# A 96-byte pad among the constants of a transformer-block kernel

## The chip, the core and the metric

The kernel runs on one core of a Trainium2 chip. The core's engines work side by side and wait for each other through semaphores: TensorE (PE in the profile; its weight loads stand apart as PEld), VectorE (DVE), ScalarE (ACT), GpSimd (POOL) and SyncE (SP), which issues nearly all transfers. The metric is the time of one execution on the device, in microseconds (us). Three runs of the kernel before gave 955.26, 956.42 and 956.73 us, so the median is 956.42 us.

## What is computed

One block of a transformer with adaptive layer norms, on 2048 tokens of width 512: a sliding-window attention with 32 heads of width 16 and a window of 256, and then a gated feed-forward part (SwiGLU) of width 1792. Cut to what matters:

```
mod = (silu(c) @ w_mod).reshape(1, 6, 1, 512)        # sa, ca, ga, sb, cb, gb
h = layernorm(x) * (1 + ca) + sa
q, k, v = split(h @ wqkv)                            # 32 heads of 16
p = softmax(mask(q @ k.T * 16 ** -0.5), -1)          # 0 <= i - j < 256
x = x + ga * ((p @ v) @ wo)
h = layernorm(x) * (1 + cb) + sb
x = x + gb * ((silu(h @ w1) * (h @ w3)) @ w2)
```

All of it is float32 from outside. Inside, most matrix products are made of three products of a high and a low part (`hi*hi`, `hi*lo`, `lo*hi`) in the type `F32R`.

## The kernel before

The program is a list of instructions for each engine, set in order by a planner inside the kernel (class `Sched`) with tables of numbers. The change does not touch the planner or its tables.

The work runs in four stages, which overlap at their borders:

1. **Start, to about 92 us.** The layer norm of `x` is written, turned, as `hT`. Line 703 makes the values `vS` from it: `hT` is the stationary operand (the weights that are loaded into the array), `wvh` or `wvl` the moving one (that streams through it).
2. **Attention, to about 471 us**, in 32 units (8 groups of 4 heads, 4 blocks of 512 tokens). Line 518 projects queries and keys (stationary `wq`, moving `hT`), lines 574 and 931 make scores (both operands in `ring`), line 892 multiplies by the values (stationary `vS`, moving `pt`).
3. **Output projection, 468 to 519 us**, line 1315 (stationary `o` or `x1b`, moving `wo`), with the second layer norm.
4. **Feed-forward, 514 to 950 us.** There are 2 halves of the tokens and 7 pairs of column blocks, so 14 passes. In each, line 1579 makes 84 matmuls (two column blocks, seven products of six: stationary a slice of the pass's weights, moving a tile of `b`), and line 1673 makes 48 (eight tiles of six: stationary the gated activations, moving the `w2` weights). The passes take turns between two sets of weight tiles, `WT[0]` and `WT[1]` (the index `s` of line 1579).

Where a tile lies in SBUF is set by pools, which are stacks from two sides. The pools `cst`, `ap`, `p0`, `a2` and `fp` grow from the low addresses; this text calls their tiles the **left side**. The pools `a1`, `hp` and `xp` are opened with `side="right"` and grow downwards from the high end: the **right side**. `cst` is the first pool on the left, so what is added there moves everything that the left side allocates later.

The lines that decide which side an operand is on, for the feed-forward part (`fp` is a left pool, `xp` a right one, and the names of line 1647 are tiles of `a1`, on the right):

```
1343  BB[m, k] = [fp.tile([P, BT], F32R, name=f"b{m}{k}{part}") for part in range(2)]
1345  WT[0, n] = [fp.tile([P, 7 * PH], F32R, name=f"w{n}{part}") for part in range(2)]
1346  W2.extend(fp.tile([P, 2, D], F32R, name=f"w2{part}") for part in range(2))
1355  for n, name in enumerate(("wo", "o")):
1356      WT[1, n] = [slot(f"{name}{part}", F32R, (P, KC, D), "xp").rearrange("p k c -> p (k c)")
1357                  for part in range(2)]
1579  nc.tensor.matmul(ps(bk), WT[s, n][w][:, col], BB[t, k][r],
1647  hn, ln = (("wq00", "wq10"), ("wq01", "wq11"), ("qkr", "qk0"), ("qk1", "qk2"),
1648            ("e0", "e1"), ("e2", "wqr"))[2 * t + f + (2 if last and t else 0)]
1673  nc.tensor.matmul(ps(bk), tiles[hk + (h,)][:, i * P:(i + 1) * P],
1674                   w2_of(last, y, f), start=(m == 0), stop=(m == 5))
```

In the very last pass half of line 1673's stationary tiles are those of line 1648: `e0`, `e1`, `e2` (left) and `wqr` (right).

Matmuls of each kind, by the side of their operands:

| line | stationary | moving | matmuls | sides |
|---|---|---|---|---|
| 703 | `hT` | `wvh`, `wvl` | 192 | right, left |
| 518 | `wq` | `hT` | 384 | right, right |
| 574, 931 | `ring` | `ring` | 512 + 512 | left, left |
| 1315 | `o`, `x1b` | `wo` | 192 | right, right |
| 1579, even passes | `w` | `b` | 588 | left, left |
| 1579, odd passes | `wo`, `o` | `b` | 588 | right, left |
| 1673 | `wq`, `qk`, `qkr`, `wqr` | `w` (`w2`) | 652 | right, left |
| 1673, end | `e` | `w` | 20 | left, left |

Lines 892 (`vS`, `pt`) are left, left too. The slices that the matmuls take out of these tiles start a multiple of 512 bytes into them (those of `vS` excepted, whose rows are 68 bytes apart), so an operand starts at its tile's address modulo 128.

Of the kernel before, what the change touches and what calls it, by code (L numbers as in the profile page):

```python
# [8 lines left out]
F32 = mybir.dt.float32  # L9
# [9 lines left out]
P = 128  # L19
# [349 lines left out]
def block_kernel(ctx: ExitStack, tc: tile.TileContext, x, wqk, wv, wo, w13, w2, c, crow, wmod, wmodt, out):  # L369
    nc = tc.nc  # L370

    cst = ctx.enter_context(tc.tile_pool(name="cst", bufs=1))
# [19 lines left out]
                op=ALU.add, axis=mybir.AxisListType.XY)  # L392

    modc = cst.tile([P, 4, KC], F32, name="modc")

    o_dr = [drm.tile([NQ * P, BT], F32, name=f"o_dr{b}") for b in range(NB)]
    g_dr = drm.tile([2, D], F32, name="g_dr")
# [1412 lines left out]
```

## Time and profile before

| | |
|---|---|
| median of three runs | 956.42 us |
| profiled execution, its own time | 956.27 us |
| its span, first to last instruction | 954.6 us |
| outside the span | 1.67 us |
| feed-forward, first to last matmul | 513.6 to 949.9 us |
| share of the span that PE is busy | 98% |
| share of PE in the chain that ended last | 86% |
| mean granted clock of PE | 0.998 |

The span is what the profile's rows explain; the 1.67 us around it are added to every sum. A matmul's own duration in the profile overlaps the next one's, since matmuls are pipelined; what one costs in a stream is the **step**, the time from its start to the start of the next. The timeline of PE gives it: it merges neighbours of one kind ("x6") and tells where each group starts.

### The profile page before, as it was taken

How to read it: one execution, taken by the hardware profiler on the slowest of the kernel's cores; microseconds unless marked ns; L12 is line 12 of the kernel's file. 1: busy time of each engine (PE TensorE's matmuls, PEld its weight loads, DVE VectorE, ACT ScalarE, POOL GpSimd, SP SyncE). 2: the span in 40 equal slices, each digit the busy share in tenths (PEclk: the TensorE clock that was granted, in tenths of full speed). 3: DMA queues.
4: the chain of work that ended last, by engine and by line, in shares of the span. 5: the costliest groups of instructions: out<-in, count | busy, mean ns of one | idle time of the engine just before them, and what ended most of it. 6: DMA issues, size and time to landing. Idle time of an engine off the chain costs nothing.

```text
span 954.6 us, 17091 instructions
## 1 busy us (share of the span) xinstructions
PE 937.3 (98%) x5296; PEld 714.9 (75%) x5296; DVE 734.3 (77%) x2065; ACT 561.1 (59%) x1263; POOL 498.9 (52%) x721
## 2 busy tenths in 40 slices
PE   8999999999999999998999999999999999999998
PEld 4678777777777677775688788888888888888886
DVE  8884989898989898998468765666679766667555
ACT  6533878787878787876779833433456333433230
POOL 3230877787878686867544655444866222221320
PEclk9999999999999999999999999999999999999999
DMA  9521444444544444437893555466684421322002
GB/s 327 191 73 40 132 170 146 147 145 147 167 159 146 146 146 145 135 129 232 240 277 101 176 162 191 137 185 221 221 279 144 149 82 57 99 84 76 23 23 88
DMA packets 81561, 141.64 MB, mean 148 GB/s; under 512 B 10555, under 2 KB 23227, under 8 KB 81470
## 3 DMA queue, kind: packets, MB, share of 16 engines
q1 hardware_dynamic: 81180, 140.29, 45.4%
q8 instruction: 42, 0.69, 0.3%
q14 instruction: 49, 0.40, 0.1%
q10 hardware_dynamic: 290, 0.27, 0.1%
HBM read 85.73 MB, written 34.61 MB: 126 GB/s over the span
## 4 chain that ended last, share of the span: by engine, by line
PE 86%; POOL 4%; DVE 3%; DMA 3%; ACT 2%; issue 1%; SPq 1%; POOLq 0%; ACTq 0%; DVEq 0%
PE st L1579 12%; PE mx L1579 10%; PE pj L518 8%; PE mx L574 7%; PE st L931 7%; PE mx L1673 7%; PE po L892 7%; PE st L1673 5%; PE pj L1579 3%; PE po L1579 3%; PE mx L703 2%; PE po L1673 2%; PE st L1315 2%; PE pj L1673 2%; PE mx L1315 2%; PE st L703 2%
## 5 line engine op out<-in xcount | busy, mean ns | idle before, releaser
L581 DVE CUSTOM_DVE_ANT_0 junk<-mx,mskq 128x384 bf16<-128x384 f32 (+1 forms) x482 | 242.1, 528 | 23.8 <-PE mx L574 22.3
L931 PE MATMUL st<-ring 100*128 100x384 f32 (+2 forms) x484 | 146.2, 343 | 1.0 <-ACT pt L952 0.4
L574 PE MATMUL mx<-ring 96*128 96x384 f32 (+2 forms) x482 | 144.6, 340 | 1.7 <-ACT pt L943 0.6
L959 POOL TENSOR_SCALAR_AFFINE_SELECT pt<-pt 128x256 f32<-128x256 f32 x268 | 108.7, 408 | 51.7 <-ACT pt L952 38.3
L518 PE MATMUL pj<-hT,wq 128*128 128x512 f32 x384 | 132.1, 403 | 0.0
L952 ACT ACTIVATE pt<-st 128x256 f32<-128x256 f32 x255 | 91.4, 387 | 36.6 <-DVE st L949 28.5
L574 PEld LDWEIGHTS mx<-ring 96*128 96x128 f32 x482 | 88.0, 189 | 31.1 <-DVE mt L581 21.1
L931 PEld LDWEIGHTS st<-ring 100*128 100x128 f32 x484 | 90.2, 189 | 18.8 <-issue 6.7
L1623 POOL TENSOR_TENSOR t<-t,t 128x512 f32<-128x512 f32 x28 | 41.6, 1487 | 115.5 <-DVE t L1611 108.4
L892 PE MATMUL po<-pt,vS 128*17 128x256 f32 (+2 forms) x1408 | 97.4, 387 | 2.7 <-ACT os L999 1.1
L536 POOL TENSOR_TENSOR qk<-qkr,qk 128x512 fp32r<-128x512 f32 x64 | 82.9, 1295 | 10.4 <-ACT qkr L524 9.0
L1170 POOL TENSOR_TENSOR w<-w,w 128x512 fp32r<-128x512 f32 (+2 forms) x35 | 51.1, 1471 | 59.0 <-ACT w L1169 58.5
L1611 DVE TENSOR_TENSOR t<-st,t 128x512 f32<-128x512 f32 x55 | 37.9, 690 | 51.4 <-PE st L1579 38.5
L518 PEld LDWEIGHTS pj<-hT,wq 128*128 128x128 f32 x384 | 71.3, 189 | 7.7 <-issue 0.9
L949 DVE COPY_PREDICATED st<-later,st 128x128 f32<-128x128 uint8 x255 | 68.8, 292 | 7.9 <-PE st L931 4.7
L892 PEld LDWEIGHTS po<-pt,vS 128*17 128x17 f32 x1408 | 32.3, 96 | 48.5 <-issue 19.3
L1579 PE MATMUL st<-b,w 128*128 128x512 f32 x234 | 59.1, 391 | 0.0
L943 ACT ACTIVATE pt<-st 128x384 f32<-128x384 f32 (+2 forms) x113 | 47.1, 433 | 14.9 <-DVE st L939 13.7
L976 POOL TENSOR_SCALAR_AFFINE_SELECT sm<-sm 128x256 f32<-128x256 f32 x109 | 42.1, 409 | 24.1 <-ACT sm L966 20.0
L1579 PE MATMUL mx<-b,w 128*128 128x512 f32 x204 | 51.7, 391 | 0.0
L1579 PEld LDWEIGHTS st<-b,w 128*128 128x128 f32 x234 | 43.9, 188 | 9.5
L1651 ACT ACTIVATE qkr<-g 128x512 fp32r<-128x512 f32 x13 | 8.2, 633 | 66.5 <-DVE g L1607 66.5
(349 smaller groups left out, 2139.7 us busy)
## 6 DMA issues: line engine op xcount, KB each, us to landing
ring<-qk SPq DMA_DIRECT2D x192, 128.0 KB
o_dr<-os SPq DMA_DIRECT2D x32, 256.0 KB
w<-wsum SPq DMA_DIRECT2D x14, 512.0 KB
w<-w2g SPq DMA_DIRECT2D x14, 512.0 KB
jb<-in_w SPq DMA_DIRECT2D x24, 256.0 KB
vS<-in_wmodt SPq DMA_DIRECT2D x22, 256.0 KB
wraw<-in_w SPq DMA_DIRECT2D x7, 768.0 KB
w<-wraw SPq DMA_DIRECT2D x14, 384.0 KB
```

The lines of the kernel that those rows point to most:

```text
L518: nc.tensor.matmul(v["ps"], WQ[g][w][:, n // 3], hTp(i, n // 3, b * BT, BT), start=(n == 0), stop=(n == 3 * KC - 1))
L536: nc.gpsimd.tensor_tensor(out=v[n], in0=v["raw"], in1=v[1].bitcast(F32), op=ALU.subtract)
L574: nc.tensor.matmul(v[i][:, :n], queries(NS, a, gq, 1), keys(NS, hh, a, k0, gq + 1 - k0), start=True, stop=True)
L581: nc.vector.tensor_tensor_reduce(out=junk[:, :n], in0=v[i][:, :n], in1=mskq[:, 3 * P - n:], scale=1.0, scalar=-3e38, op0=ALU.add, op1=ALU. ...
L892: nc.tensor.matmul(po[32 * i:32 * i + DH + 1, qb * P:(qb + nq) * P], vS[:, kb, 4 * g + i], pts[i // 2][:, i % 2, c0:c0 + nq], start=first, ...
L931: nc.tensor.matmul(ps[:, :nq], keys(NM, hh, a, kb, 1), queries(NM, a, kb, nq), start=True, stop=not plus)
L949: nc.vector.copy_predicated(ps[:, 0], later, ps[:, 2])
L952: nc.scalar.activation(pt_of(j, a)[:, hh, :2], v[j, a, hh][:, :2], AF.Exp, scale=SCALE)
L959: nc.gpsimd.affine_select(out=pt[:, :, 2 * m], in_=pt[:, :, 0], **w)
L1170: sch.op(eng, lambda: on_eng(eng).tensor_tensor(out=lo(), in0=src(), in1=hi().bitcast(F32), op=ALU.subtract), tt(eng, n), key, kl + kh, kl ...
L1579: nc.tensor.matmul(ps(bk), WT[s, n][w][:, col], BB[t, k][r], start=start and c == 0, stop=stop and c == 5, skip_group_check=True)
L1673: nc.tensor.matmul(ps(bk), tiles[hk + (h,)][:, i * P:(i + 1) * P], w2_of(last, y, f), start=(m == 0), stop=(m == 5))
```

## The change

One tile is added to the pool of constants, right behind `modc`. No instruction reads or writes it.

```
@@ -392,6 +392,8 @@
                 op=ALU.add, axis=mybir.AxisListType.XY)
 
     modc = cst.tile([P, 4, KC], F32, name="modc")
+
+    cst.tile([P, 24], F32, name="edge")
 
     o_dr = [drm.tile([NQ * P, BT], F32, name=f"o_dr{b}") for b in range(NB)]
     g_dr = drm.tile([2, D], F32, name="g_dr")
```

24 floats are 96 bytes in each partition. Every engine keeps the same instructions in the same order with the same waits; what differs is that each tile which the left side allocates after this line lies 96 bytes higher (685 buffers of the program, counted with their reuse). The right side, the constants before the line, PSUM and DRAM stay where they are. Line numbers below the pad grow by two.

Start addresses in a partition, and their rest modulo 128:

| tiles | side | before | rest | after | rest |
|---|---|---|---|---|---|
| `ident` | left, before the pad | 16512 | 0 | 16512 | 0 |
| `vS` / first `b` | left | 17344 | 64 | 17440 | 32 |
| `ring` | left | 52160 | 64 | 52256 | 32 |
| `WT[0]`: first `w` | left | 74688 | 64 | 74784 | 32 |
| `w2` | left | 103360 | 64 | 103456 | 32 |
| `wvh` | left | 106560 | 64 | 106656 | 32 |
| `h32`, `xt` (stage 1) | left | 135584, 123296 | 32 | 135680, 123392 | 0 |
| `hT` / `x1a` | right | 141920 | 96 | 141920 | 96 |
| `WT[1]`: first `wo` | right | 158304 | 96 | 158304 | 96 |
| `qk2`, `wq00` | right | 207456, 211552 | 96 | 207456, 211552 | 96 |

So a matmul with both operands on one side has them at the same rest, before and after. One with operands on both sides has them 32 bytes apart modulo 128 before, and 64 after.

More of the change, by code (lines that the diff above doesn't have):

```diff
@@ L394, in block_kernel @@
     modc = cst.tile([P, 4, KC], F32, name="modc")
+    cst.tile([P, 24], F32, name="edge")
     o_dr = [drm.tile([NQ * P, BT], F32, name=f"o_dr{b}") for b in range(NB)]
```

## The prediction

> **What bounds the kernel now.** I read the page first: the span, the engines' shares and the chain.
>
> ```profile
> span 954.6 us, 17091 instructions
> PE 937.3 (98%) x5296; PEld 714.9 (75%) x5296; DVE 734.3 (77%) x2065; ACT 561.1 (59%) x1263; POOL 498.9 (52%) x721
> PE 86%; POOL 4%; DVE 3%; DMA 3%; ACT 2%; issue 1%; SPq 1%; POOLq 0%; ACTq 0%; DVEq 0%
> ```
>
> PE is nearly always busy and carries 86% of the chain that ended last. A busy PE can still hide waits, so I cut the span into windows next (columns: the window, its length, then busy us of PE, PEld, DVE, ACT, POOL with instructions, PE's clock, DMA share, GB/s).
>
> ```profile
> 100.00:200.00 100.00, 99.39 (x750) 73.02 (x752) 91.28 (x393) 80.47 (x229) 78.50 (x147) 1.00 0.48 156
> 600.00:700.00 100.00, 100.00 (x440) 81.11 (x439) 67.27 (x87) 40.47 (x65) 52.71 (x53) 1.00 0.63 206
> 700.00:800.00 100.00, 100.00 (x433) 81.07 (x432) 75.03 (x95) 48.43 (x79) 41.95 (x26) 1.00 0.43 143
> 800.00:900.00 100.00, 100.00 (x433) 81.05 (x433) 65.08 (x87) 35.58 (x56) 24.73 (x18) 1.00 0.22 68
> ```
>
> In the feed-forward windows PE never pauses, PEld and DVE are busy 81% and 65 to 75%, and the clock is full. There a nanosecond more or less on a matmul is a nanosecond on the end. In attention DVE is at 91% as well, so less of a faster matmul would come through. The change alters no instruction; it can only act through how long instructions take. So the third view is PE's timeline, for the step of a matmul (start us, busy us, then the group).
>
> ```profile
> 697.06 1.52 PE L1579 MATMUL mx<-b,w 128*128 128x512 f32 x6
> 698.42 1.52 PE L1579 MATMUL po<-b,w 128*128 128x512 f32 x6
> 709.30 1.53 PE L1579 MATMUL mx<-b,w 128*128 128x512 f32 x6
> ...
> 489.06 2.88 PE L1315 MATMUL po<-wo,x1b 128*128 128x512 f32 x12
> 491.78 0.39 PE L1315 MATMUL st<-wo,o 128*128 128x512 f32 x1
> ...
> 551.88 1.56 PE L1579 MATMUL mx<-b,o 128*128 128x512 f32 x6
> 553.28 0.63 PE L1673 MATMUL mx<-w,qkr 128*128 128x512 f32 x2
> 568.68 1.56 PE L1673 MATMUL st<-w,wq 128*128 128x512 f32 x6
> ```
>
> This is the finding on which all rests. All these matmuls have one shape, and nothing waits. With both operands on the **left**, nine groups of six take 709.30 - 697.06 = 12.24 us, 226.7 ns a matmul. With both on the **right**, twelve take 491.78 - 489.06 = 2.72 us, again 226.7 ns. With the stationary operand right and the moving one left, 72 matmuls from 551.88 to 568.68 take 16.80 us: **233.3 ns**. The crossing costs 6.7 ns. The matmul's own rows say the same:
>
> ```profile
> L1579 PE MATMUL st<-b,w x234: 387/389/398, 513.6 to 905.2; 128*128 128x512 f32 x117
> L1579 PE MATMUL st<-b,o x132: 390/394/399, 554.7 to 924.8; 128*128 128x512 f32 x132
> ```
>
> Minimum, median and maximum are ns; the median is 5 higher across. Addresses can matter here because the next weights are read while a matmul streams:
>
> ```profile
> 621.27 1.35 PEld L1579 LDWEIGHTS mx<-b,o 128*128 128x128 f32 x6
> 621.50 1.56 PE L1579 MATMUL mx<-b,o 128*128 128x512 f32 x6
> ```
>
> The load for the group's first matmul starts 0.23 us, one step, ahead of it: with the matmul before. Two streams read SBUF at once, one from each operand. By the table of addresses they start at the same rest modulo 128 where the step is 226.7 ns (rest 64 on the left, 96 on the right: the rest itself does not matter, being equal does), and 32 bytes apart where it is 233.3 ns. The change makes these 64 apart.
>
> The Trainium skill, page "TensorE: Matmul & The Clock Gate", section "Step-by-step: what each phase is for", says that PE has two independent read ports, so that loading the next weights takes no read bandwidth from the running matmul. By that rule the two steps would be equal and the change would do nothing (956.3). Rows 697.06 to 709.30 against 551.88 to 568.68 speak against it: they differ by 6.7 ns, though the rule allows no difference.
>
> **The change part by part.** What 64 bytes apart costs, no row of a steady stream shows. I bound it. The nearest rows are 0 apart (226.7 ns) and 32 apart (233.3 ns). If the cost repeats every 64 bytes, 64 is the same as 0 and the 6.7 ns go. If it repeats every 128 and grows with the distance, 64 is twice as far as 32 and costs 6.7 ns more: 240.0. In between lies no effect. I take 226.7: after the change every operand of these matmuls, left or right, has the rest 32 modulo 64, which is how the right-right pairs stand today, and these run at 226.7. This is a choice between two periods that no row decides, and the chances below say so.
>
> *Feed-forward.* Seven of 14 passes have their weights on the right: 588 matmuls of line 1579. Line 1673 has 672; all but the 20 of the last pass with `e` cross:
>
> ```profile
> L1673 PE MATMUL mx<-w,wq x144: 389/394/402, 561.7 to 949.9; 128*128 128x512 f32 x144
> L1673 PE MATMUL pj<-w,e x5: 387/393/397, 939.0 to 940.0; 128*128 128x512 f32 x5
> ```
>
> That is 588 + 652 = 1240 matmuls by 6.67 ns = **8.3 us**, all of it on the path, by the three windows with PE at 100.00 of 100.00. As a check, 1240 x 233.3 + 608 x 226.7 ns = 427 us of the 436 from 513.6 to 949.9; transposes and the projection's last matmuls fill most of the rest. Left-left groups between crossings should gain a little too, as they need some steps to settle:
>
> ```profile
> 717.66 1.55 PE L1579 MATMUL mx<-b,w 128*128 128x512 f32 x6
> 719.06 1.56 PE L1673 MATMUL mx<-w,wq 128*128 128x512 f32 x6
> ```
>
> This left-left group lies between two crossing ones and takes 1.40 us, not 1.36. Most left-left groups follow each other, so I add nothing for it; were all 588 of them such, it would be 3.9 us, which bounds it.
>
> *Start.* Line 703 crosses as well: 192 matmuls, 1.3 us at most. Before 30 us the chain is loads and DVE work, and later PE waits now and then, so I take half, **0.6 us**.
>
> ```profile
> L703 PE MATMUL mx<-wvh,hT x72: 387/396/498, 20.4 to 92.0; 128*128 128x512 f32 x72
> L518 PE MATMUL pj<-hT,wq 128*128 128x512 f32 x384 | 132.1, 403 | 0.0
> 238.21 0.51 PE L574 MATMUL mx<-ring 96*128 96x384 f32 x2
> 238.56 0.52 PE L931 MATMUL st<-ring 100*128 100x384 f32 x2
> 238.91 0.34 PE L574 MATMUL mx<-ring 96*128 96x384 f32 x1
> ```
>
> *Attention.* Line 518's operands share a side, and so do those of lines 574 and 931, but they alternate, so the weights loaded during one line's matmul lie on the other side. Their steps are no steady stream (175 ns for 384 columns in the last rows, with waits around). If all 384 matmuls of line 518 gained 6.7 ns it would be 2.6 us; with DVE at 91% and PE's runs broken up I take a tenth, **0.3 us**.
>
> *Other engines.* Their durations show no such dependence:
>
> ```profile
> L1611 DVE TENSOR_TENSOR t<-st,t 128x512 f32<-128x512 f32 x55 | 37.9, 690 | 51.4 <-PE st L1579 38.5 <-ACT w L1169 5.3 <-ACT wo L1169 4.6
> L1678 DVE TENSOR_TENSOR x1b<-mx,x1b 128x512 f32<-128x512 f32 x21 | 14.5, 692 | 11.4 <-PE mx L1673 11.3
> L697 DVE TENSOR_TENSOR hT<-h,hT x16: 680/693/1801, 18.4 to 81.0; 128x512 fp32r<-128x512 f32 x16
> L1169 ACT ACTIVATE w<-w 128x1024 fp32r<-128x1024 f32 x14 | 14.7, 1051 | 1.5 <-DMA w<-wsum 1.5
> L1169 ACT ACTIVATE wo<-wo 128x1024 fp32r<-128x1024 f32 x7 | 7.4, 1055 | 4.0 <-DMA wo<-wsum 4.0
> ```
>
> DVE's add takes 690 ns on left tiles and 692 on right ones; `hT<-h,hT`, whose inputs lie 64 apart already, has a median of 693. ACT's copy takes 1051 and 1055. So nothing there. Transfers are hidden behind a full PE from 514 us on; at the start some are on the chain:
>
> ```profile
> 4.62 5.53 DMA vS<-in_wmodt
> 10.17 4.47 DMA wqr<-in_wqk
> ```
>
> No view parts a transfer's time by its target's address. A tenth of these 10.0 us, 1 us either way, is my bound, and I take nothing.
>
> **Sum:** 8.3 + 0.6 + 0.3 = 9.2 us off the profiled execution's 956.27: **947.0 us**. That execution is 0.15 below the median of 956.42, so it stands for the runs as it is.
>
> **The rivals.**
>
> *No effect*: the 6.7 ns belong to the two sides being far from each other and not to the rest modulo 128, or 64 costs what 32 does. For it: sides and rests go together in every pair of the trace. Time: 956.3.
>
> *Slower*: the cost grows with the distance, 240.0 ns at 64. For it: a step 32 bytes away from equal cost 6.7 ns. Against it: the argument modulo 64. Then 1240 x 6.67 = 8.3 us more, and 0.6 at the start: 965.2. It is slower as soon as the crossing step passes 234.8 ns, 1.5 ns over today's (1240 x 1.5 = 1.9 us). A weaker form: a tile's own rest counts after all, the crossings stay as they are, and left-left pairs, now at rest 32, take 233.3: 588 x 6.67 = 3.9 us more, 960.2.
>
> *More than that*: equal rests may not be the cheapest place. If 64 apart is below 0 apart by as much as 32 is above, the crossing step is 220.0 ns: 1240 x 13.3 = 16.5, with the start some 17.5: 938.8. A row that speaks for room below 226.7: 128 columns more cost 226.7 - 175 = 52 ns, 0.40 a column, so some 20 ns of a 512-column step are not streaming.
>
> The Trainium skill, page "TensorE: Matmul & The Clock Gate", section "Back-to-back issue gap", gives a stream N / 2.4 + 2.5 ns a matmul, 215.7 at N = 512. If crossing pairs fell to that, the estimate by the page is 1240 x 17.6 = 21.8 us, some 934. No steady group here shows a step under 226.7.
>
> **How the numbers follow.** About 0.2%, 1.9 us, is what a measurement of this kernel tells from none. As forecast (944 to 951): 0.54. More than that (931 to 944): 0.08. No effect (954.4 to 958.3): 0.13. Slower (958.3 to 967): 0.25, in half of it under 963. Faster by over 0.2%: 0.62; within: 0.13; slower: 0.25. The range goes from 943 to 963 and leaves out most of the deeper case and the worse half of the slower one, about 2 in 10.
>
> **What would show it.** In the changed kernel's timeline, groups of six with `b,o`, `b,wo` or `w,qk` should start 1.36 us apart, as `b,w` does, and medians of lines 1581 and 1675 should all be near 389 ns; the `b,w` groups themselves should keep 1.36. Groups at 1.40 mean no effect, at 1.44 the slower rival, at 1.32 or less the deeper one. If the crossing groups reach 1.36 and the time does not fall by 8 us, then PE waits for something that it outran, most likely the weights' split (lines 1171 and 1172) or the gates on DVE, and idle time would stand before PE from 514 us on. If `b,w` leaves 1.36, the rest itself counts, and the reading of the two equal sides was wrong.

## The result, and the profile after

| | before | after |
|---|---|---|
| median | 956.58 us (12 runs, 955.26 to 958.29) | 956.38 us (12 runs, 954.67 to 958.24) |
| profiled execution, its own time | 956.27 us | 954.69 us |
| its span | 954.6 us | 953.0 us |
| feed-forward, first to last matmul | 513.6 to 949.9, 436.3 us | 512.0 to 948.4, 436.4 us |

After stands to before as 0.9997, with a 95% interval of 0.9989 to 1.0006: no difference that the measurement can tell. The 1.6 us between the two spans lie ahead of the feed-forward part, which starts 1.6 us earlier and is as long as it was. In the seven other executions profiled here this start lies anywhere from 511.5 to 515.1 us, so 1.6 us there say nothing of the change.

The page of the changed kernel has the same shares (span, engines, chain of waits):

```profile
span 953.0 us, 17091 instructions
PE 937.9 (98%) x5296; PEld 715.3 (75%) x5296; DVE 733.5 (77%) x2065; ACT 560.5 (59%) x1263; POOL 497.5 (52%) x721
PE 87%; DVE 4%; DMA 3%; POOL 2%; ACT 2%; issue 1%; SPq 1%; POOLq 0%; ACTq 0%; DVEq 0%
```

Its windows too. PE was not freed for anything: in the feed-forward window it is busy for 100.00 of 100.00 us with 433 matmuls, as many as before.

```profile
100.00:200.00 100.00, 99.69 (x756) 73.18 (x754) 91.72 (x395) 80.71 (x229) 78.76 (x148) 1.00 0.49 157
700.00:800.00 100.00, 100.00 (x433) 81.08 (x432) 75.26 (x96) 48.54 (x78) 41.52 (x26) 1.00 0.43 141
```

So the matmuls of the feed-forward part did not get shorter. PE's timeline of the changed kernel shows it (start us, busy us, group; the lines are two higher than before). First a stretch where the stationary operand is on the right and the moving one on the left:

```profile
553.14 1.56 PE L1581 MATMUL st<-b,o 128*128 128x512 f32 x6
...
558.74 1.56 PE L1581 MATMUL pj<-b,o 128*128 128x512 f32 x6
560.14 1.56 PE L1675 MATMUL mx<-w,wq 128*128 128x512 f32 x6
...
567.14 1.56 PE L1675 MATMUL st<-w,wq 128*128 128x512 f32 x6
...
696.86 1.52 PE L1581 MATMUL po<-b,w 128*128 128x512 f32 x6
698.22 1.52 PE L1581 MATMUL st<-b,w 128*128 128x512 f32 x6
...
707.74 1.52 PE L1581 MATMUL mx<-b,w 128*128 128x512 f32 x6
```

From 553.14 to 567.14 there are 60 matmuls in 14.00 us: **233.3 ns**, the step of before, though the operands now lie 64 bytes apart modulo 128 and lay 32 apart then. The last three rows are groups with both operands on the left, whose own rest went from 64 to 32: 48 matmuls in 10.88 us, 226.7 ns, also as before.

On line 703 (705 now) the step did move. The first two rows are from before, the last two from after:

```profile
88.51 0.63 PE L703 MATMUL st<-wvh,hT 128*128 128x512 f32 x2
92.24 0.86 PE L518 MATMUL pj<-hT,wq 128*128 128x512 f32 x3
88.86 0.62 PE L705 MATMUL st<-wvh,hT 128*128 128x512 f32 x2
92.53 0.86 PE L520 MATMUL pj<-hT,wq 128*128 128x512 f32 x3
```

Between each two rows lie the same 16 matmuls of this line: 3.73 us before, 233.1 ns each, and 3.67 after, 229.4 ns. Modulo 128 its operands went from 32 to 64 apart like those of the feed-forward part, where nothing was gained. So the distance modulo 128 cannot be all that counts.

By line (minimum, median, maximum in ns, then the first and last start):

```profile
L1581 PE MATMUL st<-b,w x234: 388/389/398, 512.0 to 903.6; 128*128 128x512 f32 x117
L1581 PE MATMUL st<-b,o x132: 392/396/398, 553.1 to 923.2; 128*128 128x512 f32 x132
L1675 PE MATMUL mx<-w,wq x144: 392/396/398, 560.1 to 948.4; 128*128 128x512 f32 x144
```

The crossing kinds keep a median above that of `b,w`. They have changed inside: before, `w,wq` ran from 389 to 402 ns, and now from 392 to 398. The pad did reach these matmuls: their single durations changed, and the mean of their steps did not.

The other engines' operations, by group and by line, last what they did (690, 693 and 1051 ns before):

```profile
L1613 DVE TENSOR_TENSOR t<-st,t 128x512 f32<-128x512 f32 x55 | 37.9, 690 | 51.4 <-PE st L1581 38.5 <-ACT w L1171 5.3 <-ACT wo L1171 4.6
L699 DVE TENSOR_TENSOR hT<-h,hT x16: 682/692/1791, 19.1 to 81.5; 128x512 fp32r<-128x512 f32 x16
L1171 ACT ACTIVATE w<-w 128x1024 fp32r<-128x1024 f32 x14 | 14.7, 1050 | 1.3 <-DMA w<-wsum 1.3
```

### The profile page after: what moved, and what is told of

Read it like the earlier page. It is cut to its first block, busy times and chain, and to the rows that moved or that the text cites. A ratio compares the mean times of both kernels' runs of the same rounds, so it can differ in the third digit from the quotient of the medians.

```text
span 953.0 us, 17091 instructions
## 1 busy us (share of the span) xinstructions
PE 937.9 (98%) x5296; PEld 715.3 (75%) x5296; DVE 733.5 (77%) x2065; ACT 560.5 (59%) x1263; POOL 497.5 (52%) x721
## 4 chain that ended last, share of the span: by engine, by line
PE 87%; DVE 4%; DMA 3%; POOL 2%; ACT 2%; issue 1%; SPq 1%; POOLq 0%; ACTq 0%; DVEq 0%
PE st L1581 12%; PE mx L1581 10%; PE pj L520 8%; PE mx L576 8%; PE st L933 8%; PE po L894 7%; PE mx L1675 7%; PE st L1675 5%; PE pj L1581 3%; PE po L1581 3%; PE mx L705 2%; PE po L1675 2%; PE st L1317 2%; PE pj L1675 2%; PE mx L1317 2%; PE st L705 2%
## 5 line engine op out<-in xcount | busy, mean ns | idle before, releaser
L520 PEld LDWEIGHTS pj<-hT,wq 128*128 128x128 f32 x384 | 71.2, 189 | 7.5 <-issue 0.9
## 6 DMA issues: line engine op xcount, KB each, us to landing
w<-wsum SPq DMA_DIRECT2D x14, 512.0 KB
w<-w2g SPq DMA_DIRECT2D x14, 512.0 KB
```

The costliest lines, as they stand in the source:

```text
L520: nc.tensor.matmul(v["ps"], WQ[g][w][:, n // 3], hTp(i, n // 3, b * BT, BT), start=(n == 0), stop=(n == 3 * KC - 1))
```

## The experiments

What is left open by the result: why in the feed-forward part pairs on one side take 226.7 ns and crossing pairs 233.3, both at 32 and at 64 bytes apart modulo 128. Three answers fit these rows so far. The *side*: two operands far from each other are dearer, whatever their rests. The *rest modulo 128*: equal is cheap and everything else costs the same. A *longer period*: equal has to mean equal modulo 256, or more; then the crossing pairs stood 160 apart before and 64 after, and neither is 0. In the first three kernels the distance is varied and the sides are parted from the rests. The last three were made once these had been read. In all of them nothing but addresses changes (the one with 416 bytes also has one semaphore instruction more on GpSimd). Times are compared with the kernel before, measured again beside each group. The edits are shown against the changed kernel, so each first takes its 96 bytes out. Line numbers are one lower than those of the changed kernel where the pad is among the constants.

The distance is, here and below, the stationary operand's start minus the moving one's, modulo 256. By the table of addresses `wo` and `wq` have the rest 96, `b` and `w` before the change 192, `wvh` 64, and each pad adds its bytes to what lies behind it.

### A pad of 32 bytes: equal modulo 128

```
     modc = cst.tile([P, 4, KC], F32, name="modc")
-
-    cst.tile([P, 24], F32, name="edge")
+    cst.tile([P, 8], F32, name="edge")
```

> The pad behind modc is 32 bytes instead of 96, so both sides have the rest 96 modulo 128: 0 apart. Theory A (a step is 226.7 ns where the operands' rests modulo 128 are equal, and 233.3 where they are not, whatever the distance): the crossing groups of six (b,o; b,wo; w,qk) start 1.36 us apart instead of 1.40, and the time falls by 8 to 9 us, to some 948. Theory B (what costs 6.7 ns is that the operands lie on two sides, far apart; the rest modulo 128 is nothing): the groups stay at 1.40 and the time at 956. Left-left groups stay at 1.36 under both.

Measured: 954.89 us (11 runs) against 955.83 (21 runs), ratio 0.9985, interval 0.9976 to 0.9994. The crossing pairs now stand at equal rests modulo 128, 128 apart modulo 256. PE's timeline, first near the end of line 704 (703 before), where `hT` is stationary, and then in the feed-forward part:

```profile
88.32 0.62 PE L704 MATMUL st<-wvh,hT 128*128 128x512 f32 x2
...
90.36 0.62 PE L704 MATMUL mx<-wvh,hT 128*128 128x512 f32 x2
...
551.73 1.56 PE L1580 MATMUL mx<-b,o 128*128 128x512 f32 x6
...
568.47 1.54 PE L1674 MATMUL st<-w,wq 128*128 128x512 f32 x6
```

In the feed-forward part twelve groups, 72 matmuls, take 16.74 us: 232.5 ns. Equal modulo 128 is not enough, so this theory falls for the crossing pairs of the feed-forward part. But line 704 crosses too, and there (its `wvl` matmuls between the rows counted) 9 matmuls take 2.04 us, 226.7 ns. (Shortly behind a small matmul of `ident`, from 86.24 to 88.32, the 9 ahead of these take 2.08 us, 231.1 ns.) With the pad, `wvh` has the rest 96 and `hT` has 96: they are equal modulo 256 as well, with one operand on each side. So being on two sides does not by itself cost the 6.7 ns. The ratio is worth 1.4 us; 192 matmuls of line 704 by 6.6 ns and 1240 by 0.8 ns would give 2.3 at most, and not all of line 704 runs with PE full.

### A pad of 64 bytes

```
-    cst.tile([P, 24], F32, name="edge")
+    cst.tile([P, 16], F32, name="edge")
```

> The pad is 64 bytes, so the left side has the rest 0 and the right side 96: the weights on the right lie 96 above (or 32 below) the moving operand modulo 128, the one distance not yet seen in a steady stream. Theory A: crossing groups stay at 1.40 us, no change of time. Theory B: the same. A cost that grows with the distance one way round would show here as 1.44 or, going back to zero, less than 1.40. Left-left groups, now at rest 0, stay at 1.36 under A and B; if a tile's own rest counted they would move.

One run: 958.17 us. The crossing pairs are 96 apart; the pairs on the left have the rest 0.

```profile
559.09 1.57 PE L1580 MATMUL st<-b,o 128*128 128x512 f32 x6
...
570.34 1.56 PE L1674 MATMUL st<-w,wq 128*128 128x512 f32 x6
...
701.41 1.52 PE L1580 MATMUL st<-b,w 128*128 128x512 f32 x6
702.77 1.52 PE L1580 MATMUL mx<-b,w 128*128 128x512 f32 x6
```

Here 48 crossing matmuls take 11.25 us, 234.4 ns, while `b,w` groups keep 1.36 us. A distance of 64, 96, 128 or 160 all cost about the same, in no order with the distance. The own rest of a pair does not matter, 0 included.

### A pad between two tiles of the left side

Here `w` and `w2` are moved and `b` is not: pairs that share a side come to stand apart.

```
-    cst.tile([P, 24], F32, name="edge")
...
+            fp.tile([P, 8], F32, name="edge")
             for n in range(2):
                 WT[0, n] = [fp.tile([P, 7 * PH], F32R, name=f"w{n}{part}") for part in range(2)]
```

The new line stands ahead of the first pair of weight tiles, behind the `b` tiles.

> No pad among the constants. A 32-byte pad in the pool fp between the b tiles and everything behind them: b stays at rest 64, the w and w2 tiles and the e and t tiles go to 96, the right side's rest. So line 1579's left-left pairs (588) get operands 32 apart on one side, and line 1673's pairs across the sides (652) get operands 0 apart. Theory A: the groups b,w go from 1.36 to 1.40 us and the groups w,qk and w,wq from 1.40 to 1.36; b,o and b,wo stay at 1.40; the time changes by (588 - 652) x 6.67 ns = -0.4 us, so not by what can be told. Theory B: nothing moves, b,w at 1.36 and all that cross at 1.40.

Measured: 959.07 us (10 runs) against 955.83, ratio 1.0028, interval 1.0017 to 1.0040: slower by 0.3%. The timeline of the pairs that share the left side, `b,w`, now 32 apart, and of the crossing ones, `b,o` 160 and `w,wq` 128 apart:

```profile
553.25 1.56 PE L1580 MATMUL st<-b,o 128*128 128x512 f32 x6
...
567.26 1.56 PE L1674 MATMUL st<-w,wq 128*128 128x512 f32 x6
...
694.90 1.56 PE L1580 MATMUL pj<-b,w 128*128 128x512 f32 x6
...
708.90 1.56 PE L1580 MATMUL mx<-b,w 128*128 128x512 f32 x6
```

Ten groups of `b,w` take 14.00 us: 233.3 ns, the crossing price, between two neighbours on one side. Ten crossing groups take 14.01 us, 233.5 ns. By line, with the first and last start of the feed-forward part (511.9 to 950.6, 438.7 us, which is 2.4 more than before):

```profile
L1580 PE MATMUL st<-b,w x234: 392/395/399, 511.9 to 905.9; 128*128 128x512 f32 x117
L1674 PE MATMUL mx<-w,wq x144: 390/393/404, 560.3 to 950.6; 128*128 128x512 f32 x144
```

The price of pulling the same-side pair apart came as expected; the gain that was expected from `w,wq`, equal modulo 128, did not. This settles the side: it is the distance, on one side or across. It speaks against 128 a second time.

### A pad of 160 bytes: equal modulo 256

```
-    cst.tile([P, 24], F32, name="edge")
+    cst.tile([P, 40], F32, name="edge")
```

> The pad behind modc is 160 bytes. Seen so far: a step of 226.7 ns stood only where the operands' starts are equal modulo 256 (and 512), and equal modulo 128 alone was not enough (the 32-byte pad left the feed-forward's crossing pairs 128 apart modulo 256, at 232 to 233 ns, while line 703's pairs, which it made equal modulo 256, fell to 227). With 160 bytes the b, w, w2 and ring tiles get the rest 96 modulo 512, as the right side has. Theory C (equal modulo 256 is what it takes): the crossing groups of six start 1.36 us apart; 1240 x 6.67 ns = 8.3 us come off, with some us in attention 944 to 948. Theory B (crossing the sides costs by itself, and line 703 is another case): groups at 1.40, time 955 to 956. Line 703's pairs come to lie 128 apart modulo 256 here and should stay near 233 under C.

Measured: **947.21 us** (4 runs) against 957.27 (7 runs), ratio 0.9899, interval 0.9883 to 0.9916. The crossing pairs have the rest 96 on both sides. Timeline, lines and a window:

```profile
553.46 1.52 PE L1580 MATMUL st<-b,o 128*128 128x512 f32 x6
...
567.06 1.52 PE L1674 MATMUL st<-w,wq 128*128 128x512 f32 x6
```

```profile
L1580 PE MATMUL st<-b,w x234: 388/389/393, 512.7 to 896.4; 128*128 128x512 f32 x117
L1674 PE MATMUL mx<-w,wq x144: 388/389/389, 560.3 to 939.9; 128*128 128x512 f32 x144
L704 PE MATMUL mx<-wvh,hT x72: 390/393/505, 20.9 to 92.5; 128*128 128x512 f32 x72
```

```profile
700.00:800.00 100.00, 100.00 (x443) 82.81 (x442) 76.57 (x98) 46.71 (x75) 39.79 (x26) 1.00 0.43 140
```

Sixty crossing matmuls take 13.60 us, **226.7 ns**; every `w,wq` lies between 388 and 389 ns, where before they ran from 389 to 402. In the same window PE is just as full and does 443 matmuls in place of 433. The feed-forward part goes from 512.7 to 939.9, 427.2 us: 9.1 less than before. Line 704 now stands 128 apart and its median is 393.

### The same by 416 bytes, ahead of the feed-forward tiles alone

In this one the crossing pairs are equal modulo 256 but 256 apart modulo 512, and nothing ahead of the feed-forward tiles is moved. The new line is the first allocation of that pool, ahead of the `b` tiles.

```
-    cst.tile([P, 24], F32, name="edge")
...
+            fp.tile([P, 104], F32, name="edge")
```

> No pad among the constants; 416 bytes at the head of the pool fp, so that only the feed-forward's left tiles move, to the rest 352 modulo 512: equal to the right side's 96 modulo 256, and 256 apart modulo 512. Period 256: crossing groups at 1.36 us, the span 8 us shorter than before, 945 to 947. Period 512: groups stay at 1.40 and the span at 953 to 955. Theory B: the same as period 512.

One run: 947.73 us.

```profile
552.22 1.52 PE L1580 MATMUL mx<-b,o 128*128 128x512 f32 x6
...
568.54 1.52 PE L1674 MATMUL st<-w,wq 128*128 128x512 f32 x6
```

Seventy-two matmuls in 16.32 us, 226.7 ns. So 256 is enough and 512 is not needed. By line:

```profile
L1580 PE MATMUL st<-b,w x234: 388/389/398, 514.2 to 897.9; 128*128 128x512 f32 x117
L1674 PE MATMUL mx<-w,wq x144: 388/389/390, 561.7 to 941.4; 128*128 128x512 f32 x144
```

The feed-forward part goes from 514.2 to 941.4, 427.2 us, as with 160 bytes, though only its own tiles were moved.

### All three crossing lines equal

A pad of 32 bytes, and a tile of 128 bytes moved from the pool `ap` to the constants. That shifts the tiles of the feed-forward part by 160 bytes, and `wvh`, which lies behind the moved tile in the first stages, by 32, so that line 704 becomes equal too.

```
-    cst.tile([P, 24], F32, name="edge")
+    cst.tile([P, 8], F32, name="edge")
...
-    later = ap.tile([P, P], mybir.dt.uint8, name="later")
+    later = cst.tile([P, P], mybir.dt.uint8, name="later")
```

> As the 160-byte pad, but the extra bytes are made of a 32-byte pad and of the tile later (128 bytes), moved from the pool ap to the constants, so that wvh, wvl and the pt tiles also get the rest 96 modulo 256. Theory C: as with 160 bytes, and line 703's 192 matmuls fall to 227 too, up to 1.3 us more: 943 to 947. Theory B: 955 to 956.

Measured: **946.05 us** (4 runs), ratio 0.9888, interval 0.9869 to 0.9906.

```profile
L1674 PE MATMUL mx<-w,wq x144: 388/389/389, 558.9 to 938.5; 128*128 128x512 f32 x144
L704 PE MATMUL mx<-wvh,hT x72: 387/389/499, 20.3 to 90.9; 128*128 128x512 f32 x72
```

Line 704 has a median of 389, and its first and last `wvh` matmuls shown start 70.6 us apart, against 71.6 with the pad of 160. In the totals that one microsecond is not told apart: the two intervals overlap. This kernel has the lowest median of the study, with 32 bytes added.

### The steps, all together

| kernel | same side `b,w`: distance, step | crossing `b,o` and `w,wq`: distance, step | line 703 with `wvh`: distance, median | ratio to before |
|---|---|---|---|---|
| before | 0, 226.7 ns | 160, 233.3 ns | 32, 396 ns | |
| the change (96) | 0, 226.7 | 64, 233.3 | 192, 394 | 0.9997 |
| 32 | 0, 226.7 | 128, 232.5 | 0, 389 | 0.9985 |
| 64 | 0, 226.7 | 96, 234.4 | 224, 396 | one run |
| 32, ahead of `w` | 32, 233.3 | 160 and 128, 233.5 | 32, 396 | 1.0028 |
| 160 | 0, 226.7 | 0, 226.7 | 128, 393 | 0.9899 |
| 416, ahead of `b` | 0, 226.7 | 0, 226.7 | 32, 396 | one run |
| 32 and the moved tile | 0, 226.7 | 0, 226.7 | 0, 389 | 0.9888 |

The medians of line 703 do not show its steps: 394 ns at 192 lies closer to the 396 of before than its step does. Over the last matmuls of that line the step was 233.1 ns at 32 before and 229.4 at 192 after, by the rows in the section on the result. So 192, which no feed-forward pair had, costs less than half of what the other distances cost, and a distance modulo 256 that is not 0 need not cost the full 6.7 ns.

## Why the prediction was wrong

The forecast was 947.0 us and the kernel takes 956.4. One step failed: the choice of the period by which the cost repeats. The changed kernel's own rows show it, and the runs with 32, 160 and 416 bytes show what stands in its place.

**What bounds the kernel: right.** Feed-forward is bound by PE, and a nanosecond of a matmul is a nanosecond on the end. With 160 bytes the crossing steps fell by 6.7 ns, the feed-forward part by 9.1 us and the whole by 10.1 (947.21 against 957.27). No wait took the gain back: in the window shown PE stays at 100.00 of 100.00, so neither the weights' split nor the gates on DVE were outrun.

**The two steps, 226.7 and 233.3 ns: right as measured, wrong as read.** That "the rest itself does not matter, being equal does" holds in every kernel, once equal means equal modulo 256. But the prediction gave the distances modulo 128, where the crossing pairs are 32 apart before. Modulo 256 they are 160 apart before and 64 after, and the same-side pairs 0. All rows of before fit both, and the modulus was assumed without a row.

**The choice between two periods: the step that failed.** "I take 226.7" took a period of 64 over one of 128, and the prediction said itself that no row decides between them. Neither is the true one. With the operands 64 apart, so equal modulo 64, the feed-forward step is 233.3, and equal modulo 128 gives 232.5; equal modulo 256 gives 226.7. The feed-forward term of 8.3 us therefore came as nothing (436.3 us before, 436.4 after). Its size is about right for a pad that makes the operands equal modulo 256; this pad does not. Line 703 did gain, by less than the forecast's 6.7 ns: 3.7 ns a matmul in the rows shown, at most 0.7 us for its 192, which the total does not show.

**The terms, where the effect is there.** With 160 bytes the 8.3 us came as 9.1. The rest may be groups of `b,w` between crossing ones, which the prediction bounded by 3.9 and left at nothing: the one it shows took 1.40 us, and with 160 bytes the group between the same two neighbours takes 1.36 (713.00 to 714.36). Line 703's 0.6 us is not told apart from scatter in time: from first to last start its `wvh` matmuls take 71.0 and 70.6 us in the two kernels with distance 0, and 71.2 to 71.6 in the three with the distance of before; its step did fall to 226.7. The 0.3 us of attention stay unproven: the border at the feed-forward part scatters by more (511.5 to 515.1 us).

**Other engines and transfers at nothing: right**, by the rows of DVE and ACT after.

**The rivals.** *No effect* is what happened, at its price of 956.3, in its second form, that 64 costs what 32 does (modulo 256: that 64 costs what 160 does). Its first form, that the sides are far apart, is refuted: far sides ran at 226.7 with 160 bytes, and one side at 233.3 with the pad ahead of `w`. *Slower by distance* is refuted: the feed-forward step is 233.3 ns at 64, not 240.0. Its weaker form, a tile's own rest, falls by the `b,w` groups, which take 226.7 at the rests 192, 32, 224, 0 and 96 modulo 256. *More than that* is refuted as far as these distances go: no kernel shows a steady group under 226.7 ns. The Trainium skill, page "TensorE: Matmul & The Clock Gate", gives the 215.7 ns for back-to-back matmuls in the section "Wait — 56ns, not 53.3ns?"; the section that the prediction names, "Back-to-back issue gap", calls its formula that of an isolated matmul. No steady group here reached 215.7.

**The rule of two independent ports.** The prediction set aside what the Trainium skill, page "TensorE: Matmul & The Clock Gate", says in the section "Step-by-step: what each phase is for", that loading the next weights takes no read bandwidth from the running matmul. Taken alone, the time of the changed kernel would fit that rule. That the two operands cost each other nothing does not hold for this stream all the same: in the rows of 553.14 to 567.14 after and of 553.46 to 567.06 with 160 bytes the same 60 matmuls differ by 0.40 us, by nothing but addresses. Whether it is read bandwidth that is lost, no view shows.

**What stays open.** Why two operands equal modulo 256 go without this cost, and why 192 costs less than the other distances, was not tried; the runs show that distances and not tiles decide, and no more. Weights are loaded one step ahead (621.27 against 621.50 us, in the rows of before), so their distance could count to their own matmul's moving operand or to the one before; within the steady groups of one kind the two are at the same rest, and the runs do not part them. Only distances that are multiples of 32 bytes were run, one shape and one type.

## What to carry to other kernels

Where PE is full and the weights change with every matmul, compare the start addresses of the stationary and the moving operand modulo 256, and try a pad on one side that makes them equal; here, with one shape and type, 160 bytes of padding were worth 1.0% of the time. When an address effect is read from one kernel, write the distances for several moduli: rows that all agree with 64, 128 and 256 decide nothing, and a sweep of pads costs a run each. A pad moves every later tile of its pool, so a pair that stands well can be pushed apart, as `b,w` was by the pad ahead of `w`, and one pad need not serve every pair: 160 bytes leave line 703 128 apart.

## What the runs showed of the hardware

- The step of a matmul of 128x128 by 128x512 in `F32R`, with new weights each time, depends on the two operands' start addresses: 226.7 ns where they are equal modulo 256, 232.5 to 234.4 at the distances 32, 64, 96, 128 and 160, and 229.4 at 192 (line 705 of the changed kernel alone).
- The cost does not grow with the distance (234.4 ns at 96, 232.5 at 128, 229.4 at 192), and neither the side nor the distance in whole tiles plays a part: `wo` at 158304 against `b` at 17504, with 160 bytes, runs at 226.7 ns like two neighbours.
- Single durations can change while the mean of the steps stays: those of `w,wq` ran from 389 to 402 ns at the distance 160 and from 392 to 398 at 64, in groups of 1.40 us both times.
